# A join of two attention codes: two Ifs in place of If and Else, a hint for the jump, fewer fill matmuls

## The chip, the core and the metric

One core of one Trainium2 chip runs the whole kernel. The metric is the device time of one execution in microseconds; the time before is the median of three runs. The core has TensorE (PE; its weight loads are PEld), VectorE (DVE), ScalarE (ACT), GpSimd (POOL) and SyncE (SP), each with an instruction queue of its own, and shared transfer (DMA) engines.

## The reference

Attention with sinks and a window over 4 batches, 8 heads, 768 positions of 64 numbers; its output is the input of a layer of 8 experts, where a token goes to the expert of the largest logit, or stays with that of the token before it.

```
keep = (pos[None, :] < n_sink) | ((rel >= 0) & (rel < window))   # n_sink 4, window 128
a = exp(scores - max); a = a / (sum(a) + 1e-9)                   # masked scores are -1e9
x = matmul(a, v)                                                 # then (4, 768, 512)
for b, s:
    e = fresh_e if s == 0 or local_gate[b, s] < 0.5 else prev_e  # fresh_e = argmax(x @ w_gate)
    h = maximum(x[b, s] @ w1[e], 0)                              # 512 -> 1024
    out[b, s] = softmax(x[b, s] @ w_gate)[e] * (h @ w2[e])       # 1024 -> 512
```

## The kernel before

The numbers n_sink and window arrive at run time. The kernel holds two attention codes: a fast one for narrow windows (`attention(True)`) and a general one (`attention(False)`). The flag `narrow`, computed on the chip and loaded into a register of every engine, chooses between them with one `tc.If` and its `Else` (L1047, L1049). With these inputs the fast code runs. In the program the general code lies behind the fast code, so at the end of the fast code each engine jumps over it.

Attention goes block by block. As rows are finished, GpSimd scatters them (L380) to a buffer `xs`, ordered by expert, while routing counts the tokens of each expert into `regs`. The fast code's ending section, in which the order of instructions is written out by hand, already begins the first expert: `early_prep` (L930) gathers and transposes its first 256 rows, `early_first` (L491, result `hef`) makes six of its eight blocks of the first product, ScalarE and VectorE split each result in a high and a low part (L495, L496). Its last lines issue `FILL` (L48) pairs of matmuls on zeros (one matmul of 512 columns in this type is two in the trace, L1009), and then the last low parts:

```
                fill = bank("fill")
                for _ in range(FILL):
                    nc.tensor.matmul(fill, zrow[:, 0:P], zrow[:, 0:512], start=True, stop=True)
                low_steps(4)
                order.close()
```

The attention's pools are closed behind both codes (`at_st.close()`). Then come, again in an order written by hand, the steps that lead to the experts: SyncE issues three weight loads of 512 KB (`w_load`, L1077), two pads of zero rows (L1110), the gathers of the next rows of the first expert (`xrsn`, L1116), which read what the scatters wrote, and gathers for the second expert (`xrsm`). TensorE makes the two blocks that are left (`early_first` again, result `hl`), then products with the second weight matrix (`products`, L1295) around the transposes of the gathered rows (`high_x`, L467, tile `xpsn`). ScalarE casts weights (`highs`, L1292), VectorE makes their low parts (`low_w`, L1327), GpSimd low parts of the second expert's weights (L1353).

The eight experts follow in a Python loop; each is a `tc.Switch` (L1373) over 25 arms by the count of rows. Each Switch has hints already: `tc.switch_hint` ahead of it (L1341, and L1280 in the experts), and one for the exit of an arm (records with L1373). The records of the Switch's jumps have line L1506.

Of the kernel before, what the change touches and what calls it, by code (L numbers as in the profile page):

```python
# [17 lines left out]
ET = mybir.EngineType  # L18
# [26 lines left out]
LIMIT = 24  # L45
FIRST_F = 6
WARM = 12
FILL = 3  # L48
FIRST_P = 4
SCORED = {5: 1, 6: 1, 9: 1, 10: 1}, {41: 1, 42: 1, 43: 1, 44: 1, 45: 1, 47: 1}  # L50
CLOSED = {2: 1, 3: 1, 4: 1, 5: 1, 6: 1, 9: 1, 10: 1, 11: 1}, {38: 1, 39: 2, 41: 1, 42: 1, 43: 1, 44: 2, 46: 3, 47: 1}
# [24 lines left out]
def kernel(ctx, tc, qkd, vn, vs, w1, w2, nw, c_misc, c_ident, c_idw, c_small,  # L76
# [150 lines left out]
    with tc.issue_after(flag_op.ins) if FLAGF else ExitStack():  # L227
        for f in lead0[0:2]:
            f()

    narrow = nc.values_load(flag_i[0:1, 0:1], min_val=0, max_val=1,
                            skip_runtime_bounds_check_because="a product of comparisons")
# [225 lines left out]
    def x_steps(t, xt, j, nm, ps, tag, meta=None):  # L458
        xx = xt[0]
        meta = xt[1][:, j] if meta is None else meta  # L460
        js = slice(j * P, (j + 1) * P)
        tp = []

        def high():
            tp.append(ps.tile([P, KC, P], F32, tag=tag, name=f"xp{nm}"))
            for k in range(KC):
                nc.tensor.transpose(tp[0][:, k, :], t[:, k * P:(k + 1) * P], ident)  # L467
            for c in range(2):
                nc.vector.tensor_copy(meta[:, c:c + 1], t[:, DM + c:DM + c + 1].bitcast(I32))
            nc.scalar.copy(xx[:, :, 0, js], tp[0])  # L470

        def low():
            nc.vector.tensor_tensor(out=xx[:, :, 1, js], in0=tp[0], in1=xx.bitcast(F32)[:, :, 0, js],
                                    op=ALU.subtract)

        return high, low

    def early_prep(sfx, ps, tag):
        return [x_steps(xr0[j], early_x, j, f"{sfx}e{j}", ps, tag, late_m[j]) for j in range(NE)]
# [73 lines left out]
    def attention(fast):  # L553
# [3 lines left out]
        with ExitStack() as st:  # L557
# [58 lines left out]
            def finish(b, g, i, blk, bk, n):  # L616
                xb, lw = xb_t[b % 2], lw_t[b % 2]
                av = bk[:, 0:NPR * WX].rearrange("p (r c) -> p r c", r=NPR)
                rb = blk["rs"].unsqueeze(3)
                nc.vector.tensor_tensor(  # L620
                    out=xb[:, i, g * HG * D:(g + 1) * HG * D].rearrange("p (r t d) -> p r t d", r=NPR, t=2),
                    in0=av[:, :, 0:P].rearrange("p r (t d) -> p r t d", t=2),
                    in1=rb.broadcast_to([P, NPR, 2, D]), op=ALU.mult)
                nc.vector.tensor_tensor(
                    out=lw[:, i, g * HG:(g + 1) * HG, :].rearrange("p (r t) c -> p r t c", r=NPR),
                    in0=av[:, :, P:WX].rearrange("p r (t c) -> p r t c", t=2),
                    in1=rb.broadcast_to([P, NPR, 2, NW]), op=ALU.mult)
# [157 lines left out]
            if fast:  # L785
# [138 lines left out]
                def bank(k):  # L924
                    return ps_t.tile([P, 512], F32, tag="t", name=f"bk{nm}_{k}")

                def ending(blk, i, bk):
                    finish(b, g, i, blk, bk, nm)

                (high0, low0), (high1, low1) = early_prep(sfx, ps_s, "s")  # L930
                head_r = routing(b, 0, LAST, sfx, ps_t, "t", True)
                tail_r = routing(b, LAST, NBLK, sfx, ps_t, "t", True)
# [74 lines left out]
# [3 lines that stand above are left out]
# [34 lines left out]
                for f in range(FIRST_F):  # L1044
                    early_first(f, ps_s.tile([P, 2, 512], F32, tag="s", name=f"he{sfx}{f}")[:, 0, 0:n_e])()

    with tc.If(narrow != 0) as branch:  # L1047
        attention(True)
    with branch.Else():  # L1049
        attention(False)  # L1050
    at_st.close()

# [457 lines left out]
```

## Time and profile before

| | us |
|---|---|
| median of 3 runs | 560.55 (557.77 to 561.74) |
| the profiled execution | 561.49 |
| its span in the trace | 559.7 |
| TensorE busy | 522.3 (93%) |
| VectorE, ScalarE, GpSimd busy | 332.6, 284.2, 228.0 |

The span is the time from the first to the last instruction; 1.8 us of the profiled execution lie around it. Busy times of engines overlap. A letter q behind an engine (PEldq, ACTq) marks records of its instruction queue: jumps, waits on semaphores, register operations and DMA issues, which are not counted as busy.

### The profile page before, as it was taken

Reading aid. Unit: us, or ns where it says so; the run is one execution under the profiler, and the core shown is the slowest. Engines: PE = TensorE matmul, PEld = TensorE weight load, DVE = VectorE, ACT = ScalarE, POOL = GpSimd, SP = SyncE. Lnnn points to the kernel's source line nnn. Section 1 sums busy time; section 2 is a strip of 40 time slices with the busy share of each in tenths; the row PEclk is TensorE's granted clock in tenths of the full one; section 3 lists DMA queues with packets and bytes.
Section 4 is the critical chain, followed back from the end, with each engine's and each line's share of the span. In section 5 each row is a group of like instructions: output and inputs, shape, how many; then the busy total and the mean of one; then the engine's idle time right before and its main releaser. Section 6 shows DMA issues by size and latency. Waiting matters only on the chain. (4 is left out here: it accounts for less than half of the span.)

```text
span 559.7 us, 11841 instructions
## 1 busy us (share of the span) xinstructions
PE 522.3 (93%) x3931; PEld 444.8 (79%) x3931; DVE 332.6 (59%) x1260; ACT 284.2 (51%) x863; POOL 228.0 (41%) x194
## 2 busy tenths in 40 slices
PE   6989989999998978998999999999999799999994
PEld 3778878878887767786988889879868498889893
DVE  5567887788787866474546392815547647353321
ACT  4688888778788773441633453506315254124110
POOL 3737616563773470335530452615304444104101
PEclk8879999999999999998999999999999989999998
DMA  8555322361543143484921656649126484111000
GB/s 293 197 184 175 96 95 87 135 220 60 176 140 147 56 153 113 159 267 142 329 102 29 207 188 204 224 135 310 70 64 225 136 284 135 57 47 35 20 25 36
DMA packets 31020, 80.55 MB, mean 144 GB/s; under 512 B 3678, under 2 KB 6366, under 8 KB 30816
## 3 DMA queue, kind: packets, MB, share of 16 engines
q1 hardware_dynamic: 26064, 65.41, 35.0%
q0 software_dynamic: 4176, 12.64, 6.0%
q14 instruction: 149, 1.22, 0.7%
q8 instruction: 55, 0.90, 0.7%
q10 hardware_dynamic: 576, 0.39, 0.2%
HBM read 63.41 MB, written 16.06 MB: 142 GB/s over the span
## 5 line engine op out<-in xcount | busy, mean ns | idle before, releaser
L663 ACT ACTIVATE pef<-smf,biasf 128x264 f32<-128x264 f32 (+2 forms) x192 | 93.5, 489 | 30.2 <-DVE biasf L660 30.0
L1196 ACT ACTIVATE hq<-h 128x32 fp32r<-128x32 f32 (+4 forms) x112 | 32.0, 317 | 148.7 <-PE h L1185 95.9
L1161 DVE SCALAR_TENSOR_TENSOR hq<-h,hq 128x32 fp32r<-128x32 f32 (+4 forms) x112 | 34.4, 332 | 70.0 <-ACT hq L1196 69.7
L1234 PE MATMUL late<-w_a,hq 128*128 128x512 f32 (+2 forms) x288 | 69.3, 394 | 0.2 <-issue 0.2
L660 DVE CUSTOM_DVE_ANT_0 smf<-sf,mask 128x264 f32<-128x264 f32 (+2 forms) x192 | 66.4, 402 | 4.0 <-PE sf L648 3.0
L678 PE MATMUL tpf<-ident,pef 128*128 128x128 f32 x352 | 55.2, 292 | 7.2 <-ACT ptf L685 4.5
L1234 PEld LDWEIGHTS late<-w_a,hq 128*128 128x128 f32 (+2 forms) x288 | 50.7, 179 | 13.6 <-issue 0.7
L1216 POOL DMA_INDIRECT out_dram<-ot_d,oi_d x18 | 19.1, 1059 | 91.9 <-DVE ot_d L1215 71.9
L678 PEld LDWEIGHTS tpf<-ident,pef 128*128 128x128 f32 x352 | 38.8, 145 | 17.8 <-ACT ptf L685 8.1
L685 ACT COPY ptf<-tpf 128x512 f32<-128x512 f32 (+1 forms) x96 | 51.0, 531 | 2.4 <-PE tpf L678 2.3
L714 PE MATMUL avf<-ptf,v 128*64 128x128 f32 x704 | 50.3, 284 | 0.0
L1234 PE MATMUL late<-w_b,hq 128*128 128x512 f32 (+1 forms) x168 | 41.3, 403 | 2.3 <-issue 2.3
L380 POOL DMA_INDIRECT xs<-xb,slotf x24 | 23.7, 989 | 47.5 <-DVE exf L297 16.1
L714 PEld LDWEIGHTS avf<-ptf,v 128*64 128x64 f32 x704 | 38.5, 139 | 4.9 <-DMA v<-in_dram 0.3
L620 DVE TENSOR_TENSOR xb<-bkf,rsf 128x256 f32<-128x256 f32 x48 | 20.3, 423 | 33.1 <-ACT ptsf L695 28.7
L1234 PEld LDWEIGHTS late<-w_b,hq 128*128 128x128 f32 (+1 forms) x168 | 31.7, 191 | 9.7 <-issue 2.4
L1091 POOL TENSOR_TENSOR w_c<-raw,w_c 128x1024 fp32r<-128x1024 f32 x10 | 25.2, 2522 | 28.1 <-ACT w_c L1090 19.6
L663 ACT ACTIVATION_READ_ACCUMULATOR pef<-smf,biasf 128x1 f32 x192 | 36.3, 189 | 0.0
L1091 POOL TENSOR_TENSOR w_a<-raw,w_a 128x1024 fp32r<-128x1024 f32 x10 | 24.6, 2460 | 27.2 <-ACT w_a L1090 17.2
L1185 PEld LDWEIGHTS h<-x_a,w_c 128*128 128x128 f32 x288 | 34.9, 192 | 0.5 <-issue 0.3
L1185 PE MATMUL h<-x_a,w_c 128*128 128x256 f32 x288 | 35.1, 283 | 0.0
L604 PE MATMUL bkf<-idw,xtf 128*128 128x146 f32 x192 | 33.2, 297 | 1.3 <-DVE xtf L600 0.7
(229 smaller groups left out, 1074.8 us busy)
## 6 DMA issues: line engine op xcount, KB each, us to landing
raw<-in_dram SPq DMA_DIRECT2D x53, 512.0 KB, 5.6
raw<-in_dram SPq DMA_DIRECT2D x14, 800.0 KB, 4.6
v<-in_dram SPq DMA_DIRECT2D x7, 768.0 KB
xr_0n<-xs SPq DMA_DIRECT2D x18, 258.0 KB, 3.7
raw_w<-in_dram SPq DMA_DIRECT2D x7, 512.0 KB, 4.4
raw<-in_dram SPq DMA_DIRECT2D x10, 256.0 KB, 3.3
xs<-zrow SPq DMA_DIRECT2D x9, 258.0 KB, 7.0
xr_0r<-xs SPq DMA_DIRECT2D x8, 258.0 KB, 3.0
```

What stands on the lines that cost most here:

```text
L380: s_i = nc.gpsimd.indirect_dma_start(out=xs[:, :], out_offset=bass.IndirectOffsetOnAxis(ap=slot[:, j:j + 1].bitcast(U32), axis=0), in_=xb[ ...
L604: mm = nc.tensor.matmul(bk[:, pr * WX:(pr + 1) * WX], blk["xt"][:, pr, :], idw[:, g * NPR + pr, :], start=True, stop=True, skip_group_chec ...
L660: u["dve"] = nc.vector.tensor_tensor_reduce(out=sm[:, :w], in0=sps[:, t, :w], in1=mk, scale=-0.125, scalar=BIG, op0=ALU.add, op1=ALU.min, ...
L663: nc.scalar.activation(pe[:, h, :w], sm[:, :w], AF.Exp, bias=bias[:, t:t + 1], scale=-1.0, accum_out=z[:, h, 0:1])
L678: nc.tensor.transpose(tp[:, t, k, :], pe[:, 2 * c + t, o:o + P], ident)
L685: nc.scalar.copy(pt[:, :, 0:nt, :], tp[:, :, 0:nt, :])
L714: nc.tensor.matmul(avt[ROWS[t], pr, :], prep["v"][:, j, 2 * pr + t, :], x["pt"][:, t, k, :], start=i < 2 and pr == 0 and k == 0, stop=pr = ...
L1091: todo += [lambda s=s: lo(out=l[:, s], in0=raw[:, s], in1=h.bitcast(F32)[:, s], op=ALU.subtract) for s in ([slice(0, FF)] if eng[1] == "po ...
L1161: nc.vector.scalar_tensor_tensor(out=d[:, :, 1, :], in0=h, scalar=0.0, in1=d.bitcast(F32)[:, :, 0, :], op0=ALU.max, op1=ALU.subtract)
L1185: nc.tensor.matmul(hs, w[:, k, fs], x, start=t == 0, stop=t == len(mm) - 1)
L1196: relu = nc.scalar.activation(d[:, :, 0, :], h, AF.Relu)
L1234: nc.tensor.matmul(o, a, w, start=t == 0, stop=t == len(mm) - 1, skip_group_check=half)
```

## The change

The If with its Else becomes two Ifs, the second with a label. Ahead of `early_prep` in the fast code's ending, a hint is put on all five queues that the jump of that label is likely taken. `FILL` goes from 3 to 1.

```
-FILL = 3
+FILL = 1
...
+                tc.mark_branch_hint_location("general", "LikelyTaken", engines=[ET.PE, ET.Activation, ET.DVE, ET.Pool, ET.SP])
                 (high0, low0), (high1, low1) = early_prep(sfx, ps_s, "s")
...
-    with tc.If(narrow != 0) as branch:
+    with tc.If(narrow != 0):
         attention(True)
-    with branch.Else():
+    with tc.If(narrow == 0, label="general"):
         attention(False)
     at_st.close()
```

## Rows read from the trace of the kernel before

**Rows 1.** The head of the page: busy us, share of the span and count of instructions, and the granted clock of TensorE in 40 slices, in tenths.

```profile
PE 522.3 (93%) x3931; PEld 444.8 (79%) x3931; DVE 332.6 (59%) x1260; ACT 284.2 (51%) x863; POOL 228.0 (41%) x194
...
PEclk8879999999999999998999999999999989999998
```

**Rows 2.** Windows: for each stretch its length, the busy time of each engine (and its instructions), the mean granted clock, the busy share of the DMA engines, and GB/s. 208 is where SyncE jumps, 229.4 to 247.4 the join.

```profile
208.00:229.40 21.40, 19.17 (x170) 16.70 (x170) 13.78 (x71) 5.89 (x16) 2.94 (x3) 1.00 0.38 134
229.40:232.20 2.80, 2.73 (x8) 0.94 (x7) 1.25 (x4) 0.39 (x1) 2.13 (x3) 1.00 0.62 222
232.20:239.70 7.50, 7.47 (x43) 6.61 (x44) 2.41 (x5) 6.10 (x13) 0.79 (x1) 1.00 0.51 159
239.70:247.40 7.70, 7.59 (x35) 5.80 (x34) 6.15 (x9) 1.56 (x4) 4.71 (x2) 1.00 0.93 290
...
258.70:559.70 301.00, 287.12 (x1648) 249.42 (x1648) 145.51 (x373) 105.06 (x267) 93.98 (x55) 0.98 0.41 136
```

**Rows 3.** The jumps of line L1047 on four of the engines (one at the choice near 6 us, one at the end of the fast code): ns min/median/max, first and last start in us.

```profile
L1047 PEldq COMPARE_BRANCH  x2: 83/1809/3535, 5.8 to 228.5; - x2
L1047 ACTq COMPARE_BRANCH  x2: 43/46/49, 6.0 to 229.6; - x2
L1047 DVEq COMPARE_BRANCH  x2: 50/54/57, 6.1 to 230.0; - x2
L1047 SPq COMPARE_BRANCH  x2: 38/42/45, 8.5 to 208.0; - x2
```

**Rows 4.** The first queue records of ScalarE and VectorE behind the jump, by line (same columns), and VectorE's last steps ahead of it from the timeline (start us, us).

```profile
L1292 ACTq EVENT_SEMAPHORE  x11: 17/38/38, 232.4 to 237.0; - x11
...
L1311 DVEq TENSOR_LOAD <-regs x8: 303/308/570, 233.2 to 443.8; - x8
...
229.24 1.41 DVE L496 SCALAR_TENSOR_TENSOR hq<-hef,hq 128x256 fp32r<-128x256 f32 x4
```

**Rows 5.** GpSimd's last three scatters by line (ns min/median/max, first and last start us); the timeline of SyncE through the join (start us, us of issue); and for the tile xrsn the time from issue to landing.

```profile
L380 POOL DMA_INDIRECT xs<-xb,slotf x3: 972/974/974, 229.5 to 232.0; - x3
...
208.31 1.36 SPq L1077 DMA_DIRECT2D raw<-in_dram  x3
229.53 1.36 SPq L1110 DMA_DIRECT2D xs<-zrow  x2
237.00 1.80 SPq L1116 DMA_DIRECT2D xrsn<-xs  x3
...
DMA to landing us min/median/max: 2.7/3.0/3.3
```

**Rows 6.** Timeline of TensorE through the join (start us, us, xcount).

```profile
227.88 1.68 PE L491 MATMUL hef<-x_a,w_a 128*128 128x256 f32 x12
229.39 2.74 PE L1009 MATMUL bkf_fill<-zrow 128*128 128x512 f32 x6
232.23 3.11 PE L491 MATMUL hl<-x_a,w_a 128*128 128x256 f32 x24
235.29 4.82 PE L1295 MATMUL late<-w_b,hq 128*128 128x512 f32 x20
239.95 0.60 PE L467 MATMUL xpsn<-ident,xrsn 128*128 128x128 f32 x4
240.30 7.21 PE L1295 MATMUL late<-w_b,hq 128*128 128x512 f32 x28
```

**Rows 7.** Timeline of TensorE behind the exit of the first expert's Switch.

```profile
258.69 1.65 PE L1234 MATMUL late<-w_b,hq 128*128 128x512 f32 x3 [2.26 <-issue]
```

**Rows 8.** The Switch's jumps and hints by line (ns min/median/max, first and last start): all of TensorE's jumps; one at 245.5, one at 255.0, ScalarE's at 240.8; hints of L1341 and L1373.

```profile
L1506 PEldq COMPARE_BRANCH  x16: 308/3352/4536, 245.5 to 542.9; - x16
...
L1506 PEldq COMPARE_BRANCH  x1: 328/328/328, 245.5 to 245.5; - x1
...
L1506 PEldq COMPARE_BRANCH  x1: 3606/3606/3606, 255.0 to 255.0; - x1
...
L1506 ACTq COMPARE_BRANCH  x1: 63/63/63, 240.8 to 240.8; - x1
...
L1341 PEldq BRANCH_PREFETCH_HINT  x1: 48/48/48, 234.1 to 234.1; - x1
...
L1373 ACTq BRANCH_PREFETCH_HINT  x8: 36/40/40, 244.3 to 502.8; - x8
L1373 PEldq BRANCH_PREFETCH_HINT  x8: 36/36/41, 245.9 to 505.9; - x8
```

**Rows 9.** Two windows of 5 us, columns as in rows 2.

```profile
245.00:250.00 5.00, 4.89 (x35) 4.45 (x35) 1.86 (x11) 1.14 (x3) 2.40 (x1) 1.00 1.02 343
...
255.00:260.00 5.00, 2.74 (x16) 2.40 (x16) 3.43 (x8) 0.76 (x3) 4.68 (x4) 0.83 0.41 145
```

**Rows 10.** What the products of L1295 waited for (us, times), and the low parts of L1327.

```profile
  DVE w_b L1327: 0.7, 2
...
L1327 DVE TENSOR_TENSOR w_b<-raw,w_b x8: 677/684/2887, 238.0 to 244.4; 128x512 fp32r<-128x512 f32 x8
```

**Rows 11.** Queue records at the ends of the Switch's arms (GpSimd's, at the first arm and at all), and what GpSimd's output transfers L1216 waited for.

```profile
L1373 POOLq EVENT_SEMAPHORE  x3: 17/43/43, 254.5 to 254.7; - x3
L1373 POOLq INC_SWDGE_SEM  x8: 708/930/1183, 254.7 to 531.0; - x8
...
  POOLq L1373: 15.5, 4
```

## The prediction

> **What bounds the kernel now.** I read the engine shares and the clock line first. TensorE works for 93% of the span at nearly full clock [rows 1], so an edit counts only where it moves TensorE's own chain. The windows give that by stretch: the join of the two attention codes is the 18 us from 229.4 to 247.4, TensorE is busy there for 2.73 of 2.80, 7.47 of 7.50 and 7.59 of 7.70 us, and in the 301 us behind the first expert for 287.12 [rows 2]. So what TensorE gains or loses at the join is handed on to the end almost one for one; nothing later has slack to swallow it.
>
> The jump's own rows come next. TensorE's sequencer meets the jump over the general code at 228.5 and leaves it 3.535 us later, at 232.06; on the other engines the record lasts 38 to 57 ns [rows 3]. That is no proof that they pass freely: ScalarE's next queue record is at 232.4 against its jump at 229.6, VectorE's at 233.2 against 230.0 [rows 4], so both stand still for 2.8 and 3.1 us too. GpSimd goes on with three scatters from 229.5 to 232.0, 1.25 us apart, and SyncE jumps at 208.0 and issues weight loads at 208.31: no stall on either [rows 3, 5].
>
> Then the timeline of TensorE through the join [rows 6]: the last early products end at 229.5, six fill matmuls run from 229.39 to 232.13, the first products behind the join (hl) start at 232.23, twenty products of L1295 at 235.29, the transposes of the gathered rows (xpsn) at 239.95, and 28 more products until 247.5. The transposes are tied to something else: SyncE issues the first gather xrsn at 237.00, and the shortest of these gathers lands 2.7 us later, 239.7 [rows 5]. The gather reads the rows that the last scatter writes, and that starts at 232.0.
>
> **The change part by part.**
>
> *Fill, 6 matmuls to 2.* Six took 2.74 us [rows 6], so four fewer free 4/6 of that, 1.8 us of TensorE. While its jump lasts to 232.06 this frees nothing, since the fill only covers that stall: cost 0 for the order, and a hole of 1.8 us if the jump isn't shortened. A hole of 2.26 us at the first expert's exit [rows 7] stands in a stretch whose mean granted clock is 0.83, where the stretch at 245 has 1.00 [rows 9]. [...]
>
> *The hint itself.* One instruction on each of five queues, 36 to 48 ns where the kernel already issues them [rows 8], about 20 us ahead of the jump and in a stretch with 2.2 us of idle TensorE [rows 2]: 0 to 0.05 us, nothing taken.
>
> *TensorE's jump.* Hinted jumps exist already, at the Switch of the experts. TensorE's sixteen lasted 308 ns to 4.5 us, median 3.35 [rows 8]: some come out short, 0.33 us at 245.5 after a hint at 234.1, and some not, 3.6 us at 255.0. If the new one comes out short, TensorE is at hl's waits by 228.9, and the two fill matmuls end at 229.39 + 0.9 = 230.3. hl's accumulators take banks that the attention's last steps read; the last of those, VectorE's L496, ends at 229.24 + 1.41 = 230.65 [rows 4]. That could start hl at 230.7, not 232.23: 1.5 us, with 0 as the other end.
>
> *The other engines' jumps.* For ScalarE the hinted jump at 240.8 (63 ns) was followed by nothing until 244.3 [rows 8]: a hinted jump there stalled as an unhinted one does. So a gain on ScalarE and VectorE lies between 0 and 2.8 or 3.1 us; I take half. GpSimd and SyncE have no stall to lose.
>
> *Where 1.5 us would go.* hl and the twenty products end 1.5 us earlier, at 238.6, and then TensorE waits for xrsn's landing at 239.7. Of the gain at the transposes 0.2 us is left (239.95 to 239.75). Behind them the 28 products took 7.21 us, where the twenty before took 4.82, that is 0.241 each or 6.75 for 28: 0.46 us are lost, and the waits say to what: 0.7 us in two waits for VectorE's lows L1327 [rows 6, 10]. One of those lows took 2.9 us in place of 0.68. An earlier VectorE gives up to 0.7 of that back. In all 0.65 to 0.9, so **-0.8 us** and no more.
>
> *Two Ifs in place of If and Else.* This is the part that I weigh most. With one If and its Else either code is run, and what follows may wait on counts that both arms leave. With a second If, the general code is, by program order, behind the fast code and ahead of everything later, even if jumped over; so later users of shared tiles and semaphores must wait for counts of code that hasn't run, and each engine has to make these up as it jumps. The trace of before has such make-ups where the arms of a Switch end: event-semaphore records, on GpSimd of 17 to 43 ns, and there an instruction that raises the DMA counts, 0.71 to 1.18 us [rows 11]; GpSimd's output transfers stood idle 15.5 us in 4 cases until that queue record. At this join none shows, so I bound it. Low end: 0. Nearest rows: 0.7 us on GpSimd behind the last scatter, ahead of the gather. What hangs on it is SyncE: its three weight loads L1077, issued at 208.31, reuse buffers that the general code writes too. If they have to wait for the make-ups of TensorE, ScalarE, VectorE and GpSimd, they leave no sooner than 230.7, ahead of or beside the two pads (229.53) and the gathers (237.00) on the same queue [rows 5]. They are 3 x 512 KB = 1.57 MB. The fullest row here is 343 GB/s at share 1.02 [rows 9]: 4.6 us of all transfer engines, in a stretch from 229.4 to 239.7 that has 0.38 x 2.8 + 0.49 x 7.5 = 4.7 us of them free [rows 2]. So they fit only by filling every gap, and the scatters and gathers get later. The gather is issued at 237.0 + 0.7 and lands 2.7 us on, 240.4, if nothing collides; with the scatters sharing their time (a half of the 4.6 us at the most) it lands at up to 242.7. I take 241.6 to 242.7: 1.9 to 2.9 us after 239.7.
>
> **Sum.** Transposes later by 1.9 to 2.9; minus 0.46 to 0.7 for the lows that are then ready; plus 0 to 0.85 for the clock, as TensorE would wait about 3 us: +1.2 to +3.2, taken as **+2 us**. The profiled execution took 561.49 us with a span of 559.7, so it would give 563.5; it lies 0.9 above the median of the runs (560.55), on which I put the forecast: **562.5**.
>
> **Rivals.**
>
> *A. Only the jump is shortened.* No make-up that anyone waits for; -0.8, 559.7. For it: a short hinted jump on TensorE exists. Against: the gather sets the transposes.
>
> *No effect.* The hint is lost and the make-ups cost nothing: TensorE's jump stays at 3.5 us, hl at 232.2, **560.5**, at most 561.4 with the clock's 0.85. For it: at least half of sixteen hinted jumps were long, the one at 255.0 though its hint was issued by 245.9 [rows 8]. About 340 matmuls and weight loads pass TensorE between the hint and this jump [rows 2], more than between any of those hints and jumps that I name. [...]
>
> *C. The hint fails on ScalarE and VectorE, and the make-ups hold the loads.* VectorE's make-up is then at 233.2, the loads leave there and take to 237.8 and beyond, right on top of the gather: it lands at 242.7 to 244, +3 to +4.3, **564.3**.
>
> *D, the slower one. GpSimd's make-up holds everything.* GpSimd can raise DMA counts only once its scatters have landed. The gather's issue at 237.00 tells when the last had. If products and casts behind the join wait for a count that GpSimd raises after that, they start at 237.0 + 0.7, not 232.2: +5.5, and 0 to 0.85 for the clock, **566.5**. It decides as soon as anything of TensorE's or ScalarE's first steps behind the join waits for that count. Against it: at the Switch's ends GpSimd's semaphore records stand ahead of the DMA counts (254.5 against 254.7 [rows 11]).
>
> **How the numbers follow.** Chances: forecast 0.40 (561.7 to 563.8), A 0.25, no effect 0.13, C 0.10, D 0.12. [...] The range goes from A less that, 558.0, to D's middle, 566.5. One per cent is 5.6 us, and that is what a measurement of this kernel can tell from no change: under 554.9 none of the cases reaches except by several jumps at once (0.04); above 566.2 lies most of D and a tail of C (0.10); the rest, 0.86, is within it.
>
> **What would show it.** TensorE's jump record near 228.5: 0.3 us (short) or 3.5. hl's first product: 230.7, 232.2 or 237.7 (D). The weight loads L1077: at 208 (A, no effect) or behind 230 (forecast, C). The gather's issue and the transposes: 237.7 and 241.6 to 242.7 by the forecast, unchanged in A. ScalarE's first cast: 230 to 231 if its hint works, 232.8 if not. Make-up records on GpSimd near 237. The prediction is wrong if the loads stay at 208, if the fast code itself gets slower because its order comes out differently, or if the Switch jumps move by several at once.

## The result, and the profile after

The changed kernel takes 564.57 us (median of 11 runs, 560.87 to 566.77) where the kernel before takes 560.6 in the same comparison (11 runs, 556.65 to 568.47): a ratio of 1.007, with a 95% interval of 1.0043 to 1.0096. It is 4 us slower. Ratios leave out the runs that are over 1.5% above the fastest of their kernel, so they can differ a little from those of the medians given. The forecast was 562.5, +2 us, in a range of 558.0 to 566.5. The profiled execution took 564.25, its span is 562.5.

The first fence is TensorE's timeline through the join (start us, us, what it did, how many; in brackets the idle time ahead of it and what ended it). It answers to [rows 6].

```profile
226.44 1.68 PE L491 MATMUL hef<-x_a,w_a 128*128 128x256 f32 x12
227.95 1.02 PE L1010 MATMUL bkf_fill<-zrow 128*128 128x512 f32 x2
229.80 3.10 PE L491 MATMUL hl<-x_a,w_a 128*128 128x256 f32 x24 [0.83 <-DVEq L1050]
233.18 4.82 PE L1296 MATMUL late<-w_b,hq 128*128 128x512 f32 x20 [0.28 <-DMA raw<-in_dram]
244.81 1.09 PE L467 MATMUL xpsn<-ident,xrsn 128*128 128x128 f32 x4 [6.81 <-DMA xrsn<-xs]
245.55 8.88 PE L1296 MATMUL late<-w_b,hq 128*128 128x512 f32 x28
254.26 1.90 PE L1175 MATMUL h<-x_b,w_a 128*128 128x128 f32 x16
```

The profiled executions of the versions below reach the last hef group between 224.77 and 234.41 us, so all stages are counted from its start (226.44 here, 227.88 before). hl starts 3.36 us after it, 4.35 before: the join itself is 1 us shorter. Then TensorE stands 6.81 us until the gathered rows have landed; before, it didn't wait there at all. The transposes come at 18.37 us, 12.07 before. And the 28 products take 8.88 us in place of 7.21.

Windows of 5 us (columns as in [rows 2]) show why they do:

```profile
235.00:240.00 5.00, 3.00 (x14) 2.13 (x12) 3.93 (x7) 3.44 (x8) 0.00 (x0) 1.00 0.57 224
240.00:245.00 5.00, 0.19 (x1) 0.22 (x2) 0.22 (x2) 0.37 (x1) 4.49 (x2) 0.51 0.59 177
245.00:250.00 5.00, 5.00 (x15) 4.04 (x15) 0.69 (x1) 0.59 (x1) 0.14 (x1) 0.50 0.92 283
250.00:255.00 5.00, 5.00 (x27) 4.22 (x25) 0.00 (x0) 0.00 (x0) 0.00 (x0) 0.97 0.91 314
```

In the 5 us with the hole the granted clock falls to 0.51, and in the next 5 us, of the work behind it, it is 0.50; before, the stretch at 245 had 1.00 [rows 9].

SyncE's timeline, its loads by line and what they waited for (us in total, times, longest) tell what the rows were late for (compare [rows 5]); the last two rows are GpSimd's make-up of counts, and TensorE's jump, both on the line of the second If:

```profile
229.21 3.25 SPq L1078 DMA_DIRECT2D raw<-in_dram  x3
233.53 6.20 SPq L1111 DMA_DIRECT2D xs<-zrow  x2
241.37 2.17 SPq L1117 DMA_DIRECT2D xrsn<-xs  x3
...
L1078 SPq EVENT_SEMAPHORE  x21: 17/17/19207, 209.7 to 456.9; - x21
SPq L1078 <- PEq L1050: 19.2, 1, 19.2
...
L1050 POOLq INC_SWDGE_SEM  x1: 658/658/658, 237.1 to 237.1; - x1
L1050 PEldq COMPARE_BRANCH  x1: 454/454/454, 227.4 to 227.4; - x1
```

The three weight loads, issued at 208.31 before, now wait in SyncE's queue for 19.2 us, by this view until TensorE's queue record on the line of the second If, its make-up of counts, and leave at 229.21, ahead of pads and gathers. The issues drag: from the first to the end of the last it is 3.25 us for the three loads (1.36 before) and 6.20 for the two pads (1.36). The gather goes out at 241.37, long after GpSimd had raised its counts (237.1 + 0.66).

TensorE's jump took 0.454 us, 3.535 before [rows 3]. Where the hint stands is a surprise:

```profile
L1507 PEldq BRANCH_PREFETCH_HINT  x1: 50/50/50, 5.7 to 5.7; - x1
L1507 ACTq BRANCH_PREFETCH_HINT  x1: 50/50/50, 5.8 to 5.8; - x1
L1507 DVEq BRANCH_PREFETCH_HINT  x1: 51/51/51, 5.9 to 5.9; - x1
```

It runs as the first thing behind the choice, 221 us ahead of the jump, and not at the ending section, where the source has it.

### The profile page after: what moved, and what is told of

It reads as the page before. It is cut to its first block, busy times and chain, and to the rows that moved or that the text cites. A ratio compares the mean times of both kernels' runs of the same rounds, so it can differ in the third digit from the quotient of the medians.

```text
span 562.5 us, 11878 instructions
## 1 busy us (share of the span) xinstructions
PE 519.0 (92%) x3927; PEld 442.4 (79%) x3927; DVE 328.4 (58%) x1260; ACT 283.9 (50%) x863; POOL 227.7 (40%) x194
## 5 line engine op out<-in xcount | busy, mean ns | idle before, releaser
L1235 PE MATMUL late<-w_b,hq 128*128 128x512 f32 (+1 forms) x168 | 40.0, 393 | 1.6 <-ACT hq L1197 1.6
L1235 PEld LDWEIGHTS late<-w_b,hq 128*128 128x128 f32 (+1 forms) x168 | 30.5, 184 | 8.8 <-ACT hq L1197 1.7
L1186 PEld LDWEIGHTS h<-x_a,w_c 128*128 128x128 f32 x288 | 34.8, 192 | 2.0 <-issue 1.9
L1186 PE MATMUL h<-x_a,w_c 128*128 128x256 f32 x288 | 35.2, 283 | 1.2 <-issue 1.2
```

What stands on the lines that cost most here:

```text
L1186: nc.tensor.matmul(hs, w[:, k, fs], x, start=t == 0, stop=t == len(mm) - 1)
L1235: nc.tensor.matmul(o, a, w, start=t == 0, stop=t == len(mm) - 1, skip_group_check=half)
```

## The experiments

Ratios are to the kernel before, measured beside each version on the same chip, with their 95% intervals. The table counts all stages from the start of the last hef group, from each profiled execution's timeline; "second expert" is TensorE's jump into the second expert's Switch, "end" the end of the span.

| version | ratio (95% interval) | hl | transposes | first body products | second expert | end |
|---|---|---|---|---|---|---|
| before | 1 | 4.35 | 12.07 | 19.47 | 34.03 | 331.8 |
| before, again (e13) | - | 4.84 | 12.61 | 19.52 | 34.10 | 329.2 |
| changed | 1.0070 (1.0043 to 1.0096) | 3.36 | 18.37 | 27.82 | 40.32 | 336.1 |
| changed, again (e12) | 1.0064 (1.0031 to 1.0097) | 3.36 | 18.41 | 27.35 | 37.98 | 334.1 |
| e1 no hint | 1.0038 (1.0001 to 1.0074) | 5.75 | 17.47 | 24.35 | 34.98 | 331.4 |
| e3 loads in the codes | 0.9926 (0.9890 to 0.9962) | 3.36 | 11.95 | 18.80 | 31.70 | 331.4 |
| e7 the same, no hint | 0.9936 (0.9901 to 0.9970) | 5.98 | 15.04 | 21.87 | 33.88 | 330.3 |
| e11 the same, no hint, 3 fills | 0.9969 (0.9933 to 1.0006) | 5.95 | 13.87 | 20.70 | 33.83 | 329.9 |
| e4 loads last | 1.0136 (1.0084 to 1.0189) | 3.36 | 15.18 | 25.60 | 44.95 | 342.3 |
| e5 before, loads held | 1.0093 (1.0058 to 1.0129) | 4.37 | 18.29 | 27.54 | 38.18 | 335.6 |
| e10 before, loads in the codes | 1.0003 (0.9975 to 1.0030) | 4.36 | 12.14 | 19.75 | 34.30 | 333.0 |
| e2 before, 1 fill | 0.9987 (0.9953 to 1.0021) | 4.85 | 13.87 | 20.70 | 33.65 | 335.8 |
| e6 order exchanged, 1 fill | 0.9990 (0.9955 to 1.0025) | 2.64 | 11.10 | 17.95 | 30.62 | 332.5 |
| e9 changed, hole filled | 0.9970 (0.9935 to 1.0005) | 3.36 | 17.67 | 24.58 | 35.22 | 325.7 |

**e5: hold the loads in the kernel before.** The theory's one mechanism, alone.

```
-    for c in range(3):
-        w_load(NCH + c)
+    cast0 = nc.scalar.copy(h2(0, 2)[:, halves[0]], second_raw[0][:, halves[0]])
+    for c in range(3):
+        w_load(NCH + c, cast0)
```

(`cast0` is ScalarE's first cast behind the join, which `highs(0)` then leaves out.)

> The kernel before, If with Else and three pairs of fill matmuls, in which only the three weight loads behind the join are made to wait for ScalarE's first cast behind it (232.8 in the trace of before). Theory 'held loads': this wait alone brings the loss: the loads leave near 233.5 in place of 208.3, pads and gathers come behind them, the transposes slip from 240 to 243 or later, and the time rises by 3 to 5 us, to 563.5 to 565.5. Rival 'made-up counts': there are none at this join, so the time stays at 560.6, within 1 us.

Measured: 565.89 us where the kernel before has 562.37. SyncE's and TensorE's timelines:

```profile
232.18 1.92 SPq L1077 DMA_DIRECT2D raw<-in_dram  x3
234.69 1.23 SPq L1110 DMA_DIRECT2D xs<-zrow  x2
242.07 1.51 SPq L1116 DMA_DIRECT2D xrsn<-xs  x3
...
244.88 1.12 PE L467 MATMUL xpsn<-ident,xrsn 128*128 128x128 f32 x4 [6.19 <-DMA xrsn<-xs]
245.65 8.65 PE L1295 MATMUL late<-w_b,hq 128*128 128x512 f32 x28
```

The same hole, the same slow products, with If and Else, without a hint and without made-up counts: the held loads are enough. What the gather waits for shows in SyncE's own waits, here and, second, in the kernel before:

```profile
SPq L1116 <- DMA xs<-zrow: 4.4, 1, 4.4
...
SPq L1116 <- DMA xs<-xb,slotf: 4.2, 1, 4.2
```

Before, it is the landing of the scatters. With the loads held it is the landing of a pad: the pads went out at 234.69, behind the loads, and the gather 7.4 us after them.

**e3: move the loads into the two codes.** The mechanism taken out of the changed kernel.

```
+                with tc.issue_after(xr_op[-1].ins):        # at the end of each attention code
+                    for c in range(3):
+                        nc.sync.dma_start(stage[1 + c], w1[1, c * P:(c + 1) * P, :])
...
-    for c in range(3):
-        w_load(NCH + c)
```

(`xr_op[-1]` is the last gather of the first rows; `stage[1 + c]` is the buffer that `w_load` fills.)

> The changed kernel with the three weight loads of line 1078 taken from behind the join and issued at the end of each attention code, behind the gathers of the first rows. Theory 'held loads': they leave near 207 us, the queue of SyncE is free for pads and gathers, the gather xrsn is issued at 237 to 238 (GpSimd's raised counts cost it 0.7 us), lands at 240 to 241, TensorE's hole of 6.8 us shrinks to 1 to 3, and the time falls by 3 to 5 us from the changed kernel, to 560 to 561.5. Rival 'made-up counts': the records with which the engines make up counts are themselves what the gather waits for, whatever lies on the queue: the transposes stay behind 243 and the time stays within 1 us of 564.6.

Measured: 558.73 us where the kernel before has 562.37. The profiled execution took 563.95 us and reached its last hef group only at 230.70, so its stages are read here and not its span. SyncE's and TensorE's timelines, and between them GpSimd's make-up of counts:

```profile
210.29 2.29 SPq L1016 DMA_DIRECT2D raw<-in_dram  x3
235.05 1.45 SPq L1118 DMA_DIRECT2D xs<-zrow  x2
239.86 1.46 SPq L1124 DMA_DIRECT2D xrsn<-xs  x3
...
L1057 POOLq INC_SWDGE_SEM  x1: 658/658/658, 239.0 to 239.0; - x1
...
242.65 0.63 PE L468 MATMUL xpsn<-ident,xrsn 128*128 128x128 f32 x4 [0.41 <-DVE w_b L1333]
243.03 6.64 PE L1303 MATMUL late<-w_b,hq 128*128 128x512 f32 x28
```

The hole is gone (0.41 us, and for another reason), though every engine still makes up its counts. From the start of the last scatter to the issue of the gather it is 5.0 us here (234.84 to 239.86), 4.98 before (232.02 to 237.00) and 10.8 in the changed kernel (230.58 to 241.37). The rival falls: the made-up counts are not what the gather waits for.

**e10: the same move in the kernel before**, edit as in e3 on If and Else, three fills.

> The kernel before (If with Else, three pairs of fill matmuls, no hint) with the three weight loads issued at the end of each attention code in place of behind the join. They leave near 208 in both. Theory 'the loads gain only what two Ifs had taken': no change from the kernel before, within 0.4%. Rival 'the placing inside the codes is worth something by itself': 3 to 4 us faster, as the two versions with two Ifs and the loads inside were.

Measured: 560.42 against 560.31. As the theory had it: moved in this way, the loads give nothing by themselves.

**e4: loads behind the gathers.**

```
-    for c in range(3):
-        w_load(NCH + c)
     for e in range(2):
         pad(e)
...
     rows1 = [x_rows(r, f"sm{j}") for j, r in enumerate(lead_rows(1))]
+    for c in range(3):
+        w_load(NCH + c)
```

> The changed kernel with the same three loads still behind the join, but issued after the pads and the six gathers. Theory 'held loads': what hurts is that the loads stand ahead of the gathers; the gather xrsn is issued at 237 to 238 and lands by 241, TensorE's hole shrinks to 1 to 3 us, the loads leave at 241 and land by 247, which holds ScalarE's and GpSimd's steps on w_c for the second expert, off TensorE's path: 560.5 to 562.5. Rival 'made-up counts': no difference from the changed kernel, 564 to 565.

Measured: 571.34 against 562.37. Both theories missed. ScalarE's timeline:

```profile
237.57 2.19 ACT L1293 CAST w_b<-raw 128x512 fp32r<-128x512 f32 x4 [1.28 <-DVE hq L496]
251.27 2.38 ACT L1293 CAST w_c<-raw 128x512 fp32r<-128x512 f32 x4 [11.51 <-DMA raw<-in_dram]
253.56 0.58 ACT L470 CAST x_b<-xpsn 128x512 fp32r<-128x512 f32 x1
```

The casts of these weights stand ahead of the cast of the gathered rows in ScalarE's written order. I had called them off TensorE's path; they block it. The loads can come late for neither side: ahead of the gather they hold the rows, behind it the casts. The gather itself left 8.2 us after the last scatter's start, better than 10.8 but not 5.0. SyncE's waits show 2.3 us of it for the scatters' landing; the rest is open.

**e1: no hint.** The changed kernel without the line of the hint.

> The changed kernel without its hint: two Ifs, one pair of fill matmuls. Theory 'the hint shortens the jumps': without it TensorE's jump at the end of the fast code takes 3 to 3.6 us again (0.45 with the hint), ScalarE's and VectorE's next records come 2.5 us or more after their jumps (0.4 to 0.6 with it), and since the held weight loads wait for the counts that these engines make up, they leave 1.5 to 2.5 us later than 229.2, so the time is 1 to 2 us above the changed kernel: 565.5 to 566.5. Rival 'the placing of the code shortens them' (with two Ifs what is jumped to lies otherwise): the jumps stay short without the hint, and the time is that of the changed kernel, 564.6.

Measured: 563.83 against 562.37. The jump on TensorE, and what followed there:

```profile
L1049 PEldq COMPARE_BRANCH  x1: 4100/4100/4100, 225.7 to 225.7; - x1
...
230.52 4.56 PE L491 MATMUL hl<-x_a,w_a 128*128 128x256 f32 x24 [3.22 <-DVEq L1049]
234.92 4.72 PE L1295 MATMUL late<-w_b,hq 128*128 128x512 f32 x20
242.24 0.63 PE L467 MATMUL xpsn<-ident,xrsn 128*128 128x128 f32 x4 [2.60 <-DMA xrsn<-xs]
242.62 6.66 PE L1295 MATMUL late<-w_b,hq 128*128 128x512 f32 x28
```

So the hint shortens the jump: 4.1 us without it, 0.45 with it; ScalarE's make-up comes 2.8 us after its jump without it and 0.5 with it (226.7 to 229.5; 228.5 to 229.0). The time did not follow. The loads left 5.2 us after the last hef group's start (2.8 with the hint), and yet the transposes come 0.9 us earlier: SyncE's two pads took 1.83 us to issue, 6.20 with the hint. TensorE's waiting is split in 3.22 and 2.60 us; hl pays for the first (4.56 us, 3.10 with the hint), and the 28 products run at a granted clock of 1.00 (240 to 250). By the intervals this version can't be told from the changed kernel; it is not the 1 to 2 us slower that I expected.

**e9: fill the hole** with twelve matmuls on zeros.

```
     products(range(0, 5))
+    hole = ps_x.tile([P, KC, P], F32, tag="x", name="hole").rearrange("p k c -> p (k c)")
+    for _ in range(6):
+        nc.tensor.matmul(hole, zrow[:, 0:P], zrow[:, 0:512], start=True, stop=True)
     high_x()
```

> The changed kernel with six more fill calls (twelve matmuls, about 5.1 us) on TensorE between the first twenty products and the transposes that wait for the gather, where it had a hole of 6.8 us and the granted clock fell to 0.5. Theory 'the hole costs twice, by its length and by the clock behind it': the clock stays at 1.0, the 28 products behind the transposes take 6.6 us in place of 8.9, and the time falls by about 2 us from the changed kernel, to 562 to 563 where that has 564.6. Rival 'only the landing counts': the products' time is made good later, and the time stays within 0.7 us of the changed kernel.

Measured: 559.45 against 560.93.

```profile
240.78 5.31 PE L1363 MATMUL hole<-zrow 128*128 128x512 f32 x12
247.07 0.66 PE L467 MATMUL xpsn<-ident,xrsn 128*128 128x128 f32 x4 [0.98 <-DMA xrsn<-xs]
247.48 6.66 PE L1296 MATMUL late<-w_b,hq 128*128 128x512 f32 x28
```

The landing is hardly better (transposes at 17.67, 18.37 in the changed kernel), but the products take 6.66 us in place of 8.88 (granted clock 1.00 from 240 to 255), and the first body products come 3.2 us earlier. The hole costs twice. By the two ratios the time fell by more, 1.0% or 5.6 us; in the profile the rest lies in later stages (TensorE's idle time ahead of the experts' products of L1186 for which the profile shows no wait is 2.7 us in all, 8.4 and 8.8 in the two executions of the changed kernel). What does it was not separated.

**e2: one fill in the kernel before** (`FILL = 1`, nothing else).

> The kernel before, If with Else, with one pair of fill matmuls in place of three and nothing else. TensorE still sits in its jump for 3.5 us, now with a hole of about 1.8 us in front of hl, which starts 4.3 us after the start of the last hef group as before. Theory 'the fill only covers the jump': no change, within 1 us of the kernel before. Rival 'the fill keeps the clock': the hole lowers the granted clock and the time rises by 1 us or more.

Measured: 560.63 against 560.93, no difference that the interval shows. In the profile there is one: a hole of 2.32 us, a granted clock of 0.88 and 0.78 in the two windows from 230 to 240, hl in 4.27 us in place of 3.11, the first body products at 20.70 in place of 19.47. 1.2 us is less than this comparison resolves (its interval is 1.9 us to either side).

**e6: the general code first, the fast one in the Else**, one fill.

> One If with its Else again, but with the order of the two codes exchanged: the general code stands in the If, the fast one in the Else, one pair of fill matmuls, no hint. The far jump is now at the choice near 6 us, and at the end of the fast code nothing is jumped over. Theory: engines pass the join without a stall (hl starts 2.8 to 3.4 us after the start of the last hef group, 4.35 before), no counts have to be made up there, and the weight loads leave at 208 as before; the join gives back about 1 us. The far jump at the choice costs 0 to 3.5 us, as TensorE's first products wait for it or not: 559 to 564 where the kernel before has 562. Rival: loads held here too, as the counts of the skipped code must be known behind it: they leave behind 228 and the time is 565 or more.

Measured: 562.14 against 560.93, ratio 0.999. What the first theory had at the join shows: hl at 2.64 (a little under its 2.8), body products 1.5 us earlier, loads at 213.44 in an execution whose last hef group starts at 234.41. The price is at the choice, where TensorE now jumps far, and it is more than the 3.5 us that I had allowed:

```profile
L1047 PEldq COMPARE_BRANCH  x1: 5337/5337/5337, 5.7 to 5.7; - x1
...
11.18 1.81 PE L648 MATMUL sf<-w_a 64*128 64x128 f32 x10 [4.87 <-issue]
```

**e7 and e11: loads in the codes, no hint**, with one fill and with three.

> The version with the three weight loads inside the two attention codes (two Ifs, one pair of fill matmuls), without the hint. Theory 'the hint is worth something once the gather isn't held': TensorE's jump takes 3.5 us again and VectorE's make-up comes 3 us later, so hl starts 5.7 us after the start of the last hef group (3.4 with the hint), the twenty products end behind the landing of xrsn, and the time is 2 to 3 us above that of the hinted version. Rival 'the gather sets the transposes in any case': the time stays within 1 us of the hinted version.

> The version with two Ifs, the loads inside the two attention codes and no hint, with three pairs of fill matmuls in place of one. There the hole in front of hl was 3.45 us and the granted clock 0.83 from 230 to 240. Theory 'the fill keeps the clock under an unshortened jump': the hole is 1.5 to 2 us, the clock stays above 0.95, hl takes 3.1 us in place of 4.5, and the transposes come 1 us earlier: 0.5 to 1.5 us faster than with one pair. Rival: the landing of the gather takes the gain, no difference.

Measured: 557.74 against 560.93, and 557.92 against 560.31. By the intervals e7 can't be told from e3, though its hl starts 2.6 us later and its body products 3.1 us later: my expectation was wrong, and here too the jump's 4.0 us don't show in the time. In e11 the join goes as expected (clock 1.00, hl in 3.11 us in place of 4.48, body products 1.2 us earlier); the time can't be told from that of e7, nor, by an interval that just reaches 1, from the kernel before.

**e12 and e13: both kernels once more.**

> The changed kernel itself once more, for a second profiled execution and a ratio on this chip. Theory: the weight loads leave 2 to 3 us after the start of the last hef group, the gather lands 17 to 19 us after it, TensorE's hole in front of the transposes is 4 to 7 us and the clock behind it near 0.5; ratio to the kernel before 1.004 to 1.010. Rival 'the first profile was an odd one': hole below 3 us, clock 1.0.

> The kernel before itself once more, for a second profiled execution: which stages differ between two executions of one kernel. Theory: the join repeats within 0.5 us (hl 4.3, first body products 19.5 us after the start of the last hef group), while the first 50 us of the fast code and the stages around the experts' jumps differ by 1 to 3 us each.

The join repeats: the hole is 6.98 us (6.81), the body products come at 27.35 (27.82), against 19.52 and 19.47 before. The ratio is 1.0064. My expectation for the fast code was wrong: the two executions reach the last hef group at 227.88 and 227.76 us (226.44 and 226.46 in the changed kernel), no 1 to 3 us apart. What doesn't repeat is the rest: the two executions of the kernel before differ by 2.6 us behind the body products.

## Why the prediction was right, and where its sizes were off

**The bound, and the chain.** TensorE's chain sets the end of the join, and it hangs on the gathered rows wherever the loads are held (changed, e1, e5, e9). In the kernel before, e2, e6, e7, e10 and e11 TensorE came to the transposes without a wait, in e3 after 0.41 us for VectorE, and in e4 ScalarE's casts came on top of the wait.

**The likeliest case was the right one:** counts of the skipped code, weight loads that leave behind 229, a later gather, +2 us. Its chance was 0.40, and what was to show it showed: loads behind 230 (229.21), a short jump (0.454), transposes late. Its number did not come true as well: its own band was 561.7 to 563.8 (its upper term, 2.9 - 0.46 + 0.85, is 3.3, not 3.2). The 564.57 lies beside C's 564.3, whose condition, that ScalarE and VectorE still stall, did not arise.

**The term that was mis-sized is the gather.** I let the loads cost it 0 to 2.3 us of shared transfer time and put its issue at 237.7, GpSimd's 0.7 us behind the old one. It went out at 241.37, in an execution whose fast code ended 1.4 us earlier: 5.8 us later from the last scatter's start. The sum priced the loads' share of transfer time and GpSimd's counts, and left out the pads: they stand behind the held loads and ahead of the gather, and the gather waits for them too. In the changed kernel 9.45 us of SyncE's issues (3.25 + 6.20) come first. Long issues are not needed for the slip, though: in e5 they take 3.15 us, and the gather is as late (11.3 us after the last scatter's start), waiting 4.4 us for a pad's landing; in e1 they take 3.40, and it is 10.6. What kept SyncE between the two pads of the changed kernel is open. And GpSimd's 0.7 us, the one part of that wait that I had a row for, cost nothing (e3: 5.0 us as before). So the transposes came 6.3 us later, not 1.9 to 2.9.

**The clock** was allowed 0 to 0.85 us for a wait of 3. No run shows this term; it equals what the 5 us at 255, at a mean clock of 0.83 [rows 9], lack to 1.00. What the runs show in its place: the wait was 6.8, and behind it the granted clock was 0.50 for 5 us and the products took 2.2 us longer (8.88 against 6.66 in e9); behind e4's wait of 3.53 it was 0.66 (245 to 250), and they took 8.22; behind e1's of 2.60 it was 1.00, and they took 6.66. The 0.46 to 0.7 us that an earlier VectorE was to give back were no sure part of the sum: the 28 products take 6.64 us in e3, but 6.72 in the second execution of the kernel before too, against 7.21 in the first.

**The step that I left out halves the loss again.** I wrote that nothing later has slack. From the first body products to the second expert's jump the kernel before takes 14.56 us, the changed one 12.5 and 10.63 in its two executions, e5 10.64, e1 10.63. So 2 to 3.9 us come back. In the kernel before TensorE sits 3.6 us in the first exit's jump [rows 7, 8]; here is that jump in the two executions of the changed kernel:

```profile
L1507 PEldq COMPARE_BRANCH  x1: 2946/2946/2946, 261.9 to 261.9; - x1
...
L1507 PEldq COMPARE_BRANCH  x1: 386/386/386, 261.5 to 261.5; - x1
```

In e5 it took 0.41. By TensorE's timelines the first products behind that jump started without a wait in e1, e5, e9 and e12, whose body products come later than 24 us, and after 1.8 to 2.5 us in the seven executions where these come before 21 us (before, e13, e2, e3, e6, e10, e11). Why is open. For such jumps, turned short or long as code moves, the range reaches 1.7 us below A's 559.7; no run shows this term, and the jump above took 2946 and 386 ns in two executions of one and the same code. 8.35 us late at the first body products, the profiled execution ends 4.2 us late. Two errors, one in each direction, left the forecast 2 us short of the truth; that they cancelled as far as this was luck.

**The hint.** The doubt about ScalarE and VectorE (case C, half of the gain taken) was unfounded: with the hint TensorE's jump took 0.454 us, and ScalarE's and VectorE's make-ups come 0.5 and 0.6 us after their jumps; without it (e1) these are 4.1, 2.8 and 3.3. The rival of no effect falls as well: a hint executed 221 us and some 2,100 matmuls ahead, not the 20 us that I had counted on, still went with a short jump. Without a hint TensorE's far jump took 3.535 us in the kernel before, 4.1 in e1, 4.0 in e7 and 5.3 in e6.

**Rival A** would need the loads to stay where they were. e3 is that case, hinted: its body products come 18.80 us after the last hef group's start, 0.67 earlier than before, of the size that A worked out (0.8). Its time, 4.1 us under the kernel before, A does not explain. **Rival D** falls: hl started at 229.80, far ahead of GpSimd's counts at 237.1, 6.5 us after the start of the last scatter (230.58), which took those 6.5 us to land.

**What stays open:** why two Ifs with the loads inside (e3, e7) are 0.6 to 0.7% faster than the kernel before. The place of the loads alone is not it (e10), and the join can't be all of it (e7's is later than that of before). Up to the second expert's jump e3 is 2.3 us ahead of the kernel before, e7 0.2; where the rest lies can't be read from single executions, which in the kernel before differ by 2.7 us behind that jump.

The better version is e3 or e7, 4.1 and 3.6 us under the kernel before by their ratios (0.9926 and 0.9936), and faster than both kernels of this case.

## What to carry to other kernels

Before an Else becomes a second If, list what follows the join early, transfers above all, and ask which counts it will wait for: code that is skipped still stands in the program's order, and here the loads waited 19.2 us for its counts. With two Ifs, a load that is due at the join belongs inside each branch (e3). And a wait of TensorE can be paid twice: 6.8 us ahead of the transposes made the 28 products behind it 2.2 us longer, and 2.3 to 3.5 us ahead of hl (e2, e1, e7) made hl 1.2 to 1.5 us longer.

## What the runs showed of the hardware that I had not expected

The branch hint was issued at 5.7 us, and the jump at 227.4 us took 0.45 us, 4.1 without the hint (e1). SyncE's issues are not of constant cost: three loads took 3.25 us to issue and two pads 6.20, where each had taken 1.36; busy transfers alone don't explain it, since e5, with the same loads in flight, needed 1.92 and 1.23. And the granted clock of the first 50 us differs between executions of one kernel, 0.83 and 0.90 in the kernel before, without a difference of more than 0.12 us at the last hef group.
